# Other handover times, another hold-back rule and two other costs in the planner that orders a fused LSH-attention and expert-network kernel

## The chip, the cores and the metric

The kernel runs on one core of a Trainium2 chip. A core has five engines that run side by side, each working through its own list of instructions in the order in which they were written: TensorE (PE; its weight loads are shown as PEld), VectorE (DVE), ScalarE (ACT), GpSimd (POOL) and SyncE (SP), which here only issues transfers (DMAs). An engine waits when its next instruction needs something that another engine or a transfer has not delivered, and everything behind that instruction waits too. The metric is the time of one execution on the device in microseconds (us).

## The reference

Two stages follow each other. The first is attention in which a query may see only those keys that fall into the same hash bucket; the second is a dense two-layer network with a squared ReLU.

```python
# 4 batches, 8 heads, 768 positions, head size 64
q_bits = einsum(q, proj) > 0                 # 6 bits a row; the same for k
mask   = bucket(q)[:, None] == bucket(k)[None, :]
scores = where(mask, q @ k.T / 8, -1e9)
attn   = exp(scores - max); attn = attn / (sum(attn) + 1e-9)
x      = (attn @ v) as rows of 512           # heads side by side, 3072 rows
h      = x @ w_in                            # 512 -> 2048
out    = (s * relu(h)**2 + b) @ w_out        # 2048 -> 512
```

Everything is in float32, so the kernel splits operands of the matmuls into a high and a low part and adds the products.

## The kernel before, in words

The attention is cut into 96 *slots*: one batch, one head, one chunk of 256 queries against all 768 keys. Batch 0 is visited twice (first chunk 0 of all heads, then chunks 1 and 2); from batch 1 on each head is visited once, with its three chunks. Scores lie transposed, keys on the partitions, in three banks of PSUM, the memory that TensorE writes (128 keys by 256 queries twice in a bank).

A slot has a chain in which each step needs the one before:

- `scores`, first half: score matmuls in pairs (L523 for the exact slots at the start, L525 for all others), the maximum over keys on VectorE (L530, tile `mx`), two transposes on TensorE (L534), a second maximum on VectorE (L536, tile `nmt`), a transpose to rows on TensorE (L538), and the rows made into an operand on VectorE (L544, tile `bq` or `zhl`);
- `scores`, second half: the remaining matmuls, which also subtract the maximum (L553 or L555), and three exponentials on ScalarE (L560). Each exponential frees a bank, into which the next slot's score matmuls go.

Off that chain are `values` (cast and low part of the exponentials on ScalarE and GpSimd, L577 and L578; the matmuls with v, L584 and L585, or L582 in batch 0; the sum over keys on VectorE, L606; for every second head a reciprocal on VectorE, L622, the division on GpSimd, L623, and a transfer of the pair's result `xsb` to DRAM, `xd`, L627), the preparation of a head's queries and keys (L384 to L420), and, in the first part of the kernel, `decode`, which turns 32 blocks of the weights into split float32 (L303 to L316). VectorE's part of a decode are L306 and L307, one dependent on the other.

The second stage is `moe`: 12 chunks of 256 rows. A chunk reads its rows back (`xc<-xd`, L647), four head pairs each; then for each two of 16 blocks of the hidden size there are 24 matmuls (L660), ScalarE and GpSimd steps (L665 to L668), and 12 matmuls with w_out (L677). A chunk has 192 L660 and 96 L677 matmuls. They have the lowest priority, so they fill TensorE between the steps of the attention, earlier chunks ahead of later ones. What is left when attention ends is run alone.

None of this is emitted in program order. Every step is entered into `Plan` (L32) with its engine, an estimated cost, a priority (lower is more urgent) and what it reads and writes. `order` then plays the program through once, before anything is built: it goes from decision to decision, always for the engine that can start soonest; that engine takes, among the steps whose producers have all been placed (`open_`), the most urgent one that is ready. A step is ready when its last producer's cost and *handover time* (`HOP`; less `SAME` where both are on one engine) are over. With `LOOK` an engine may also take a more urgent step that is not ready yet but soon will be, and stays idle until then. The times that come out of this are used for one thing alone: sorted by them, the steps are emitted, and this fixes the order on each engine and on the queues. What is put down as a step's cost changes nothing in the step.

A step's priority is `pr`: slot i has 10 i; the next slot's scores are entered with 10 (i + 1) - 8, exponentials 4 less than that, values 10 i + 5, decodes 10 i + 15, the reciprocal 10 i + 25, the expert network 10000 and more. In `order`, `moved` stands for a transfer queue that moves 260,000 bytes per us.

Of the kernel before, what the change touches and what calls it, by code (L numbers as in the profile page):

```python
# [15 lines left out]
ALU = mybir.AluOpType  # L16
# [11 lines left out]
PE, DVE, ACT, POOL, SP = (mybir.EngineType.PE, mybir.EngineType.DVE, mybir.EngineType.Activation,  # L28
                          mybir.EngineType.Pool, mybir.EngineType.SP)


class Plan:  # L32
# [25 lines left out]
    def order(self):  # L58
        n = len(self.steps)
        left = [len(s[5]) for s in self.steps]  # L60
        users = [[] for _ in range(n)]
        for i, s in enumerate(self.steps):
            for d in s[5]:
                users[d].append(i)
        ready = [0.0] * n
        free = {}
        moved = 0.0
        open_ = {}
        for i in range(n):
            if not left[i]:  # L70
                open_.setdefault(self.steps[i][0], []).append(i)
        out = []
        while len(out) < n:
            best = None
            for e, lst in open_.items():
                if lst:
                    t = max(free.get(e, 0.0), min(ready[i] for i in lst))
                    if best is None or t < best[0]:
                        best = (t, e)
            t, e = best  # L80
            i = min((i for i in open_[e] if ready[i] <= t + LOOK.get(e, 0.0)), key=lambda i: (self.steps[i][3], i))
            open_[e].remove(i)
            eng, cost, fn, pr, lag, deps = self.steps[i]
            start = max(free.get(e, 0.0), ready[i])
            free[e] = start + cost
            end = start + cost + HOP[e]
            if e == SP:
                moved = max(moved, start + cost) + lag
                end += moved - start - cost
            else:  # L90
                end += lag
            out.append((start, i))
            for u in users[i]:
                ready[u] = max(ready[u], end - (SAME[e] if self.steps[u][0] == e else 0.0))
                left[u] -= 1
                if not left[u]:
                    open_.setdefault(self.steps[u][0], []).append(u)
        self.length = max(free.values())
        self.start = {i: t for t, i in out}
        return [i for _, i in sorted(out)]  # L100

HOP = {None: 0.0, PE: 0.2, DVE: 0.13, ACT: 0.2, POOL: 0.1, SP: 1.8}
SAME = {None: 0.0, PE: 0.2, DVE: 0.0, ACT: 0.05, POOL: 0.0, SP: 0.0}
LOOK = {PE: 0.0, DVE: 0.5, ACT: 0.2}


@with_exitstack
def lsh_attention_moe(ctx: ExitStack, tc, q, k, v, proj, w_in, w_out, s, b, out):  # L110
    nc = tc.nc
# [25 lines left out]
    def f32(ap):  # L137
        return ap.bitcast(F32)
# [11 lines left out]
    def dve(n, fn, r, w, pr, ns=None):  # L150
        plan.add(DVE, ((n + 64) / 960.0 if ns is None else ns), fn, r, w, pr)

    def act(n, fn, r, w, pr, more=0.0):
        plan.add(ACT, 0.13 + n / 1070.0 + more, fn, r, w, pr)

    def pool(n, fn, r, w, pr, ns=None):
        plan.add(POOL, (0.12 + n / 430.0 if ns is None else ns), fn, r, w, pr)
# [126 lines left out]
    def decode(u, pr):  # L284
        src, key = dec[u]
        box = {}

        def new():
            box["t"] = wk.tile([P, 512, 2], I32, tag=f"w{u}", name=f"raw{u}")

        def swap():
            wt[key] = wk.tile([P, 2, 512], F32R, tag=f"w{u}", name=f"w{u}")

        def raw():
            return box["t"]
        rk, wk_ = [("raw", u)], [key + (0,), key + (1,)]
        g, gk = osb[:, u % 2, :], ("os", u % 2)
        gi = g.bitcast(I32)

        x = f"e{(u - 16) // 2}"  # L300
        plan.add(None, 0.0, new, [], rk + ([] if u < 16 else AK(x) if u % 2 == 0 else KK(x)) + [("vs", x, u % 2)], pr - 5)

        plan.add(ACT, 0.1, lambda: nc.scalar.dma_start(raw(), src.rearrange("p (n t) -> p n t", t=2)), KK("e0") if u < PACE else [], rk + [("pace", u % PACE)], pr - 5, 5.0)  # L303
        act(512, lambda: nc.scalar.activation(g, raw()[:, :, 1].bitcast(F32), AF.Copy, scale=float(2.0**-112)), rk + [("pace", u % PACE)], [gk], pr)
        act(512, lambda: nc.scalar.activation(raw()[:, :, 0], raw()[:, :, 0].bitcast(U32), AF.Copy, scale=float(2.0**-29)), rk, rk, pr)
        dve(256, lambda: nc.vector.tensor_scalar(raw()[:, :, 1], gi, -2**31, None, ALU.bitwise_and), [gk], rk, pr, 0.54)  # L306
        dve(512, lambda: nc.vector.scalar_tensor_tensor(gi, gi, 3, raw()[:, :, 1], ALU.logical_shift_left, ALU.bitwise_or), rk, [gk], pr, 0.88)  # L307
        pool(512, lambda: nc.gpsimd.tensor_tensor(gi, gi, raw()[:, :, 0], ALU.add), rk, [gk], pr)
        plan.add(None, 0.0, swap, [], rk + wk_, pr)
        act(512, lambda: nc.scalar.copy(wt[key][:, 0], g), [gk], [key + (0,)], pr)  # L310
        if key[0] == "wo":
            if key[1] == 0:
                pool(512, lambda: nc.gpsimd.tensor_copy(bcs, g), [gk], ["bcs"], pr + 5)
            else:
                pool(512, lambda: nc.gpsimd.tensor_tensor(bcs, bcs, g, ALU.add), [gk], ["bcs"], pr + 5)
        pool(512, lambda: nc.gpsimd.tensor_tensor(wt[key][:, 1], g, f32(wt[key][:, 0]), ALU.subtract), [gk, key + (0,)], [key + (1,)], pr)  # L316
# [9 lines left out]
    def AK(x, r=(0, 1), g=(0, 1, 2)):  # L326
        return [("aq", x, i, j) for i in r for j in g]
# [4 lines left out]
    def KK(x, r=(0, 1, 2, 3, 4)):  # L332
        return [("ks", x, i) for i in r]
# [384 lines left out]
    for i in range(NSL):  # L718
        pr = 10.0 * i
# [15 lines left out]
        while nd[0] < min(ND, decodes(i)):  # L735
            decode(nd[0], pr + 15)
            nd[0] += 1
# [58 lines left out]
```

## Time and profile before

| | us |
|---|---|
| median of 3 runs (1116.52 to 1120.74) | 1117.24 |
| the profiled execution | 1122.19 |
| its span, first to last instruction | 1120.4 |
| TensorE busy in it | 1061.0 |
| ScalarE, GpSimd, VectorE busy | 702.5, 683.9, 657.1 |

The profile is of one execution. "Busy" is the time in which an engine had an instruction in work; matmuls are pipelined and their ends are modelled. A row of a group reads: line, engine, operation, tiles out<-in, shapes, count | busy us, mean ns of one | idle time of the engine just before these instructions, and what ended it. In the timeline a piece is: start, length, engine, line, and in square brackets the idle time before it and who ended it. A row of a stretch gives, after its bounds and length, the busy time of each engine with the number of its instructions, then the clock that TensorE was granted (1.00 is full), the share of time in which the DMA engines were busy, and GB/s.

### The profile page before, as it was taken

Reading aid. Unit: us, or ns where it says so; the run is one execution under the profiler, and the core shown is the slowest. Engines: PE = TensorE matmul, PEld = TensorE weight load, DVE = VectorE, ACT = ScalarE, POOL = GpSimd, SP = SyncE. Lnnn points to the kernel's source line nnn. Section 1 sums busy time; section 2 is a strip of 40 time slices with the busy share of each in tenths; the row PEclk is TensorE's granted clock in tenths of the full one; section 3 lists DMA queues with packets and bytes.
Section 4 is the critical chain, followed back from the end, with each engine's and each line's share of the span. In section 5 each row is a group of like instructions: output and inputs, shape, how many; then the busy total and the mean of one; then the engine's idle time right before and its main releaser. Section 6 shows DMA issues by size and latency. Waiting matters only on the chain.

```text
span 1120.4 us, 18819 instructions
## 1 busy us (share of the span) xinstructions
PE 1061.0 (95%) x6862; PEld 919.1 (82%) x6862; DVE 657.1 (59%) x807; ACT 702.5 (63%) x1377; POOL 683.9 (61%) x617
## 2 busy tenths in 40 slices
PE   8998788999999999989999999999999999999998
PEld 6665666878888888778888888888888998898987
DVE  6666576766767776766777676767776752000000
ACT  5556677766677667666767667677776765333332
POOL 5345898876777667656767676767676765222221
PEclk9888899999999999989999999999999999999999
DMA  8644454433322422332333242233233202101010
GB/s 173 160 138 129 131 138 113 131 96 86 89 73 69 133 61 73 90 88 56 78 100 91 53 130 61 76 81 98 63 81 86 70 1 85 39 19 57 1 57 19
DMA packets 99404, 94.49 MB, mean 84 GB/s; under 512 B 68528, under 2 KB 72112, under 8 KB 99312
## 3 DMA queue, kind: packets, MB, share of 16 engines
q1 hardware_dynamic: 94112, 76.24, 26.1%
q10 hardware_dynamic: 5200, 17.05, 5.0%
q8 instruction: 54, 0.88, 0.3%
q14 instruction: 38, 0.31, 0.1%
HBM read 49.81 MB, written 18.87 MB: 61 GB/s over the span
## 4 chain that ended last, share of the span: by engine, by line
PE 80%; DVE 7%; ACT 5%; DMA 3%; POOL 3%; issue 2%; SPq 0%; DVEq 0%; ACTq 0%; POOLq 0%
PE bank L660 23%; PE bank L677 21%; PE bank L555 5%; PE bank L525 5%; PE bank L582 4%; PE bank L585 4%; PE bank L584 4%; PE bank L523 2%; PE bank L534 2%; PE bank L384 2%; PE bank L612 2%; DVE mx L530 2%; DMA xd<-xsb 2%; DMA xc<-xd 1%; ACT et L560 1%
## 5 line engine op out<-in xcount | busy, mean ns | idle before, releaser
L578 POOL TENSOR_TENSOR hl<-et,hl 128x512 fp32r<-128x512 f32 x216 | 278.1, 1317 | 163.0 <-ACT hl L577 147.6
L660 PE MATMUL bank<-xc,w 128*128 128x256 f32 x2304 | 344.8, 288 | 9.5 <-DMA xc<-xd 8.0
L660 PEld LDWEIGHTS bank<-xc,w 128*128 128x128 f32 x2304 | 307.5, 191 | 20.9 <-DMA xc<-xd 9.3
L677 PE MATMUL bank<-w,ghb 128*128 128x512 f32 x768 | 256.3, 397 | 0.0
L668 POOL TENSOR_TENSOR glb<-rb,ghb 128x512 fp32r<-128x512 f32 x96 | 124.4, 1296 | 137.9 <-ACT ghb L667 130.0
L530 DVE TENSOR_REDUCE mx<-bank 128x256 f32<-128x1536 f32 x96 | 168.1, 1752 | 44.0 <-PE bank L525 25.7
L677 PE MATMUL bank<-w,glb 128*128 128x512 f32 x384 | 152.1, 400 | 0.5 <-POOL glb L668 0.5
L665 ACT ACTIVATE rb<-bank 128x512 f32<-128x512 f32 x96 | 57.1, 595 | 151.3 <-PE bank L660 148.7
L677 PEld LDWEIGHTS bank<-w,ghb 128*128 128x128 f32 x768 | 136.7, 189 | 17.2
L560 ACT ACTIVATE et<-bank 128x512 f32<-128x512 f32 x240 | 130.7, 624 | 31.2 <-PE bank L555 27.6
L606 DVE TENSOR_REDUCE zb<-et 128x256 f32<-128x1536 f32 x72 | 126.1, 1751 | 41.3 <-ACT et L560 41.0
L577 ACT CAST hl<-et 128x512 fp32r<-128x512 f32 x216 | 128.6, 661 | 0.8
L584 PE MATMUL bank<-hl,vs 128*128 128x256 f32 x432 | 121.6, 299 | 0.5 <-ACT hl L577 0.5
L525 PE MATMUL bank<-aq,ks 78*128 78x256 f32 x528 | 118.6, 308 | 1.4 <-ACT et L560 0.7
L585 PE MATMUL bank<-hl,vs 128*128 128x256 f32 x432 | 115.8, 288 | 2.9 <-POOL hl L578 2.5
L525 PEld LDWEIGHTS bank<-aq,ks 78*128 78x128 f32 x528 | 91.0, 194 | 12.6 <-ACT ex L560 2.0
L685 DVE SCALAR_TENSOR_TENSOR osb<-bank,misc,bcs 128x512 f32<-128x512 f32 x22 | 16.2, 744 | 132.4 <-PE bank L677 132.4
L585 PEld LDWEIGHTS bank<-hl,vs 128*128 128x128 f32 x432 | 82.5, 191 | 8.8 <-POOL hl L578 6.0
L555 PE MATMUL bank<-bq,ks 128*128 128x256 f32 x528 | 79.5, 287 | 9.6 <-DVE bq L544 8.3
L616 ACT ACTIVATE xpb<-bank,vmn 64x256 f32<-64x256 f32 x96 | 44.9, 468 | 69.3 <-PE bank L585 67.7
L584 PEld LDWEIGHTS bank<-hl,vs 128*128 128x128 f32 x432 | 82.1, 190 | 3.8 <-ACT hl L577 0.7
L622 DVE RECIPROCAL zpb<-zpb 128x256 f32<-128x256 f32 x48 | 83.7, 1743 | 2.3 <-ACT zpb L614 1.9
(111 smaller groups left out, 1662.9 us busy)
## 6 DMA issues: line engine op xcount, KB each, us to landing
xd<-xsb SPq DMA_DIRECT2D x48, 256.0 KB
xc<-xd SPq DMA_DIRECT2D x48, 256.0 KB
raw<-in_moe_w_in_dram ACTq DMA_DIRECT2D x16, 512.0 KB
raw<-in_moe_w_out_dram ACTq DMA_DIRECT2D x16, 512.0 KB
nat<-in_q_dram SPq DMA_DIRECT2D x32, 192.0 KB
nat<-in_k_dram SPq DMA_DIRECT2D x32, 192.0 KB
bq<-aq SPq DMA_DIRECT2D x32, 192.0 KB
out_dram<-osb SPq DMA_DIRECT2D x22, 256.0 KB
```

The lines of the kernel that those rows point to most:

```text
L525: nc.tensor.matmul(o, ks[0:HR + TPC, 0, kt], aq[0:HR + TPC, cs], start=m == 0, stop=m == 1, skip_group_check=True)
L530: dve(S * TPC, lambda: nc.vector.tensor_reduce(t, sc, AX.XY, ALU.max), [("b", b) for b in pb], [tk], pr, 1.75)
L555: nc.tensor.matmul(o, ks[:, 1, kt], bq[:, cs], start=False, stop=m == 1, skip_group_check=True)
L560: act(512, lambda p=p, z=z: nc.scalar.activation(et(z) if plain(i) else pairs(z), bank[:, pb[p]] if plain(i) else bank[:, pb[p]].rearrange ...
L577: act(512, lambda z=z, y=y: nc.scalar.copy(HL[2 * y].rearrange("p (m n) -> p m n", n=CH), pairs(z)), [("e", z)], [("hl", 2 * y)], pr)
L578: pool(512, lambda z=z, y=y: nc.gpsimd.tensor_tensor(HL[2 * y + 1].rearrange("p (m n) -> p m n", n=CH), pairs(z), f32(HL[2 * y]).rearrange ...
L584: nc.tensor.matmul(av, VS[w % 2][:, kt], HL[2 * y][:, ms], start=(kt == 0), stop=False)
L585: nc.tensor.matmul(av, VS[w % 2][:, kt], HL[2 * y + 1][:, ms], start=False, stop=(kt == NT - 1))
L606: dve(S * TPC, lambda: nc.vector.tensor_reduce(ZB, es, AX.XY, ALU.add), [("e", z) for z in range(NE)], ["zb"], pr, 1.75)
L660: nc.tensor.matmul(hp, wt[("wi", n, cc)][:, m % 2, fs], xc[:, m // 2, :], start=(cc == 0 and m == 0), stop=(cc == NC_ - 1 and m == 2))
L668: pool(2 * CH, lambda r=r, gh=gh, gl=gl: nc.gpsimd.tensor_tensor(gl, r, f32(gh), ALU.subtract), [rk, hk], [lk], MP)
L677: nc.tensor.matmul(bank[:, 6 + t, :], (gh, gh, gl)[n][:, ts], wt[("wo", f)][:, n % 2], start=(f == 0 and n == 0), stop=(f == NF - 1 and n ...
```

## The change

Only the planner's numbers and its rule of choice change; no step is added, removed or given other work.

- `HOP`, the handover time: VectorE 0.13 to 0.06 us, ScalarE 0.2 to 0.06, GpSimd 0.1 to 0.06. TensorE (0.2) and SyncE (1.8) stay.
- `SAME`, what is taken off where producer and user are on one engine, is now equal to `HOP` on these three engines, so that a dependent step follows at once in the plan. Before, 0.13, 0.15 and 0.1 us were left between them.
- `LOOK`: ScalarE's goes from 0.2 to 0. VectorE's stays 0.5 but was a time in us and is now a factor: the most urgent ready step is found first, and a more urgent one is taken in its place only if it will be ready within half the found step's cost.
- VectorE's decode steps are entered with 0.68 and 1.1 us instead of 0.54 and 0.88.

```diff
-            i = min((i for i in open_[e] if ready[i] <= t + LOOK.get(e, 0.0)), key=lambda i: (self.steps[i][3], i))
+            rank = lambda i: (self.steps[i][3], i)
+            i = min((i for i in open_[e] if ready[i] <= t), key=rank)
+            i = min((j for j in open_[e] if ready[j] <= t + LOOK.get(e, 0.0) * self.steps[i][1] and rank(j) <= rank(i)), key=rank)
...
-HOP = {None: 0.0, PE: 0.2, DVE: 0.13, ACT: 0.2, POOL: 0.1, SP: 1.8}
-SAME = {None: 0.0, PE: 0.2, DVE: 0.0, ACT: 0.05, POOL: 0.0, SP: 0.0}
-LOOK = {PE: 0.0, DVE: 0.5, ACT: 0.2}
+HOP = {None: 0.0, PE: 0.2, DVE: 0.06, ACT: 0.06, POOL: 0.06, SP: 1.8}
+SAME = {None: 0.0, PE: 0.2, DVE: 0.06, ACT: 0.06, POOL: 0.06, SP: 0.0}
+LOOK = {DVE: 0.5, ACT: 0.0, POOL: 0.0}
...
-        dve(256, lambda: nc.vector.tensor_scalar(raw()[:, :, 1], gi, -2**31, None, ALU.bitwise_and), [gk], rk, pr, 0.54)
-        dve(512, lambda: nc.vector.scalar_tensor_tensor(gi, gi, 3, raw()[:, :, 1], ALU.logical_shift_left, ALU.bitwise_or), rk, [gk], pr, 0.88)
+        dve(256, lambda: nc.vector.tensor_scalar(raw()[:, :, 1], gi, -2**31, None, ALU.bitwise_and), [gk], rk, pr, 0.68)
+        dve(512, lambda: nc.vector.scalar_tensor_tensor(gi, gi, 3, raw()[:, :, 1], ALU.logical_shift_left, ALU.bitwise_or), rk, [gk], pr, 1.1)
```

## The prediction

> **What bounds the kernel now.** I read the page first: its engine rows, the granted clock in 40 slices, and the chain that ended last.
>
> ```profile
> span 1120.4 us, 18819 instructions
> PE 1061.0 (95%) x6862; PEld 919.1 (82%) x6862; DVE 657.1 (59%) x807; ACT 702.5 (63%) x1377; POOL 683.9 (61%) x617
> ...
> PEclk9888899999999999989999999999999999999999
> ...
> PE 80%; DVE 7%; ACT 5%; DMA 3%; POOL 3%; issue 2%; SPq 0%; DVEq 0%; ACTq 0%; POOLq 0%
> ```
>
> TensorE is busy for 1061.0 of 1120.4 us. The change adds and removes no instruction, so it can only act on the other 59 us, and on the slices in which the granted clock is below 9. Next, the stretches: busy time of each engine, granted clock, DMA share.
>
> ```profile
> core 0: us, PE busy (x) PEld busy (x) DVE busy (x) ACT busy (x) POOL busy (x), PEclk, DMA share, GB/s
> 84.00:224.00 140.00, 116.15 (x608) 92.95 (x607) 94.72 (x104) 98.50 (x186) 113.00 (x92) 0.93 0.45 129
> 224.00:470.00 246.00, 235.83 (x1619) 208.99 (x1618) 174.42 (x211) 171.41 (x348) 169.15 (x156) 1.00 0.33 85
> 470.00:486.00 16.00, 10.35 (x57) 8.63 (x56) 9.25 (x12) 6.79 (x15) 6.92 (x7) 0.79 0.27 70
> 486.00:905.00 419.00, 408.58 (x2844) 365.25 (x2845) 300.24 (x351) 298.71 (x603) 294.25 (x274) 1.00 0.31 80
> 905.00:1121.00 216.00, 210.68 (x1346) 189.62 (x1344) 25.61 (x30) 79.87 (x137) 64.72 (x55) 1.00 0.11 36
> ```
>
> TensorE's idle time is 23.9 us in 84 to 224 (140 - 116.15), 10.2 in 224 to 470, 5.7 in 470 to 486, 10.4 in 486 to 905, 5.3 in the last stretch. That last stretch is nothing but expert-network matmuls that were left over. So attention that finishes earlier does not end the kernel earlier by itself: filler that is no longer run between its steps is run in the tail. The end moves by TensorE's idle and half-clock time alone.
>
> Does attention from 486 on wait for TensorE, or TensorE for attention? These are groups of that stretch; the last columns are idle time before the group and what ended it.
>
> ```profile
> L606 DVE TENSOR_REDUCE zb<-et 128x256 f32<-128x1536 f32 x45 | 78.8, 1751 | 22.3 <-ACT et L560 22.2
> L585 PE MATMUL bank<-hl,vs 128*128 128x256 f32 x266 | 71.4, 288 | 1.4 <-POOL hl L578 1.2
> L555 PE MATMUL bank<-bq,ks 128*128 128x256 f32 x264 | 38.5, 282 | 0.0
> L544 DVE SCALAR_TENSOR_TENSOR bq<-bank,ident 2x256 fp32r<-2x256 f32 x44 | 18.1, 412 | 38.1 <-PE bank L538 38.1
> L538 PE MATMUL bank<-ident,nmt 128*2 128x128 f32 x44 | 11.9, 271 | 3.0 <-ACT aq L386 3.0
> ```
>
> VectorE waits 38.1 us for the row transposes (L538), TensorE 0.0 us for what VectorE then makes of them (L555). The chain's results lie ready and wait for their turn in TensorE's written order. There the order decides, and the handover times hardly do.
>
> **The change, part by part.**
>
> *Handover times.* The planner's time from an engine's end to another's start goes to 0.06 us for VectorE (from 0.13), ScalarE (0.2) and GpSimd (0.1). What the trace has, where TensorE did stand waiting:
>
> ```profile
> 128.52 0.41 DVE L544 SCALAR_TENSOR_TENSOR bq<-bank,ident 2x256 fp32r<-2x256 f32 x1 [0.36 <-PE bank L538]
> 128.98 0.98 PE L555 MATMUL bank<-bq,ks 128*128 128x256 f32 x6 [0.51 <-DVE bq L544]
> ...
> 400.35 0.47 ACT L386 ACTIVATE aq<-bank,misc 128x256 fp32r<-128x256 f32 x1 [1.85 <-DVE nmt L536]
> 400.88 0.27 PE L538 MATMUL bank<-ident,nmt 128*2 128x128 f32 x1 [0.55 <-ACT aq L386]
> ```
>
> 128.52 + 0.41 = 128.93 to 128.98 is 0.05 us; 400.82 to 400.88 is 0.06. The new figures are right. A slot's chain has three handovers from VectorE (L530, L536, L544) and one from ScalarE (exponential to the next slot's scores): 3 x 0.07 + 0.14 = 0.35 us less per slot in the plan. TensorE's written order then has up to 0.35 us less filler between the chain steps of a slot. From 486 to 905 the trace has 45 slots (L606), 9.3 us each, so some 26 lie between 224 and 470; over those it is up to 9 us of filler not yet used when batch 1's attention ends. On the end itself: 0, by the last stretch above, except at one place, next.
>
> *The batch boundary at 470 to 486.* Filler of batch 0 is three chunks of 192 L660 matmuls, 576. The trace, L660 alone and then pieces of the timeline:
>
> ```profile
> 0.00:472.40 472.40, 97.48 (x585) 81.40 (x585) 0.95 0.42 111
> 472.40:481.10 8.70, 0.00 (x0) 0.00 (x0) 0.81 0.40 100
> ```
>
> ```profile
> 470.28 0.38 SPq L145 DMA_DIRECT2D xd<-xsb  x1
> ...
> 477.00 0.41 DVE L544 SCALAR_TENSOR_TENSOR bq<-bank,ident 2x256 fp32r<-2x256 f32 x1 [0.36 <-PE bank L538]
> ...
> 478.46 0.33 SPq L647 DMA_DIRECT2D xc<-xd  x1
> ...
> 481.15 0.58 PE L660 MATMUL bank<-xc,w 128*128 128x256 f32 x1 [4.18 <-DMA xc<-xd]
> ...
> 482.38 1.48 PE L555 MATMUL bank<-bq,ks 128*128 128x256 f32 x6
> ```
>
> At 472.4 all 576 are done, and 9 of batch 1 (its first three head pairs). The next L660 needs the fourth pair. The planner gives a transfer 0.7 us of issue, 1 us of moving and 1.8 of handover; the write to DRAM issued at 470.28 lets its read start only at 478.46. So TensorE stands 4.18 us at an L660, and the chain's L555, whose input was ready at 477.41, waits behind it until 482.38. Then the clock:
>
> ```profile
> 477.74:484.57 6.83, 3.42 (x16) 3.42 (x17) 1.32 (x3) 1.88 (x4) 1.71 (x2) 0.50 0.23 70
> 191.02:194.44 3.42, 3.42 (x12) 2.87 (x11) 0.23 (x1) 3.19 (x7) 3.42 (x3) 0.50 0.60 170
> 675.72:679.13 3.41, 2.88 (x13) 2.88 (x14) 2.35 (x3) 2.20 (x5) 3.41 (x4) 0.50 0.31 68
> ```
>
> Work that took 3.42 us at 0.50 would take 1.71 at full clock. If filler of batch 0 is left, it comes first (earlier chunks have the higher priority) and the stall is covered. Worth: 5.65 us idle in the stretch, less 0.4 that 16 us of the stretch after would have anyway (10.42 / 419 x 16), plus 1.7 for the clock: 7.0 us. Bounds: 0 (nothing left over) to 7.0. I take 7.0: some 4 us of leftover covers the 4.2 us stall, and up to 9 is offered.
>
> The rows at 191 and 675 show the clock halved by lesser stalls as well. The Trainium skill, "TensorE: Matmul & The Clock Gate", section "Why this matters for your kernels", advises against idle gaps over about 3 us, because an idle window of that length throttles the array. By that rule a new gap of 1 to 2 us would cost its own length. This trace has the half clock at 675.72, where no gap reached 3 us, so by the rows it can cost up to 1.7 us on top (half of 3.4).
>
> *Margins.* The old figures were longer than the hardware's, and so were a cushion. Where TensorE meets its producer exactly, each error of the plan now becomes a stall. From 486 on little of that is in sight (L555 0.0, L585 1.4, L538 3.0 us over 44 slots). Bounds: 0, and a doubling of the idle time from 224 to 470 and 486 to 905, +20.6. I take +1.5, near L585's 1.4, since results there wait for TensorE. The freed cushion is near the lower bound.
>
> *Holding back.* Before, an idle VectorE waited up to 0.5 us for a step of higher rank, whatever it held back. Now it waits up to half the cost of that operation: 0.875 us for 1.75 us ones, 0.55 for the second decode step, 0.34 for the first, 0.21 to 0.27 for the short ones. But the planner sees a step only once all its producers are placed, and it places the engine that can start soonest first. A step behind TensorE is therefore seen at most a TensorE cost and handover ahead: 0.43 us for L536 (0.23 + 0.2), 0.32 for L544, 0.44 for an inexact slot's L530. All are below the old 0.5. For long operations the new bound holds back nothing more there, only before steps behind an exponential (0.61 + 0.06) and behind the long exact score groups; for short ones it holds back less. And right at the end of L530, L534 is not yet placed, so L536 is not seen at all. What this costs today, in 84 to 224:
>
> ```profile
> 115.11 1.76 DVE L530 TENSOR_REDUCE mx<-bank 128x256 f32<-128x1536 f32 x1 [1.50 <-PE bank L525]
> 116.79 1.74 DVE L622 RECIPROCAL zpb<-zpb 128x256 f32<-128x256 f32 x1
> 118.45 0.36 DVE L536 TENSOR_REDUCE nmt<-bank 128x2 f32<-128x256 f32 x1
> 118.73 1.26 DVE L306 TENSOR_SCALAR raw<-osb 128x512 int32<-128x512 int32 x1
> 119.91 0.41 DVE L544 SCALAR_TENSOR_TENSOR bq<-bank,ident 2x256 fp32r<-2x256 f32 x1
> ...
> 118.87 0.27 PE L538 MATMUL bank<-ident,nmt 128*2 128x128 f32 x1 [1.44 <-DVE nmt L536]
> 120.37 1.01 PE L555 MATMUL bank<-bq,ks 128*128 128x256 f32 x3 [1.23 <-DVE bq L544]
> ```
>
> A reciprocal straight after L530 costs TensorE 1.44 us, a decode step straight after L536 costs 1.23. By the code above, both can come again. ScalarE no longer waits at all (0.2 before): an exponential may then start behind another operation, and what waits for it is the next slot's scores and L606 on VectorE. That lengthens a slot; TensorE has filler meanwhile, so 0, and without filler up to one ScalarE operation in such a slot. The stage in sum:
>
> ```profile
> L530 DVE TENSOR_REDUCE mx<-bank 128x256 f32<-128x1536 f32 x16 | 28.0, 1753 | 26.9 <-PE bank L525 22.5 <-ACT raw L305 3.5 <-PE bank L523 1.0
> L555 PE MATMUL bank<-bq,ks 128*128 128x256 f32 x81 | 13.6, 305 | 9.1 <-DVE bq L544 7.8 <-POOL bq L433 1.2
> ```
>
> 16 slots, in which TensorE waits 7.8 us for L544. At best 70% of that goes, 5.5 us, and two halved windows of 1.7: -9. At worst as much comes: +9. I take -1, nearer nothing than either, since the mechanism stays and only some cost figures come closer.
>
> *Decode costs* go to 0.68 and 1.1 us.
>
> ```profile
> L307 DVE SCALAR_TENSOR_TENSOR osb<-osb,raw 128x512 int32<-128x512 int32 x32 | 37.0, 1157 | 0.5
> L306 DVE TENSOR_SCALAR raw<-osb 128x512 int32<-128x512 int32 x32 | 21.7, 679 | 3.8 <-ACT osb L304 3.7
> ```
>
> The means agree. The plan gives VectorE 32 x 0.36 = 11.5 us more, the chip does the same work: 0. But one figure stands for different things (1.26 us at 118.73 against a mean of 0.68). The Trainium skill, "SBUF — State Buffer", names a port pair that VectorE and GpSimd take exclusively, the loser blocked for a whole instruction. By it a decode step in front of the chain costs what GpSimd's running instruction has left, which the plan does not hold.
>
> *Sum:* -7.0 + 1.5 - 1 = -6.5 us. The profiled execution took 1122.19 us, 1.8 more than its span and 4.95 more than the median of the runs shown, 1117.24; the terms are differences, so I put them to the median: 1110.7, say 1110.5 us.
>
> **The rivals.**
>
> *The boundary stays (chance 0.22).* The real slot is set by TensorE's order and by VectorE's 1.75 us blocks, and does not shorten by the plan's 0.35 us; filler runs out as before. For it: 9 of batch 1's matmuls were done already, so there was no margin at all. Then the small terms alone: 1117.24 + 0.5, 1117.7 us.
>
> *Decode steps block the chain more often (0.24): slower.* L306 and L307 now follow each other without the 0.13 us between dependent VectorE steps, and short ones are held back less. Place: 84 to 224, with little filler to cover. Price: about 1.2 us per slot (the 1.23 above); the 7.8 us of today are worth six or seven such stalls in 16 slots. Seven more are +8.4 us, one more halved window +1.7, with the boundary as before: about 1127. It decides from five more on (6 us).
>
> *The hold works where it is needed (0.14).* If the plan's new times move the reciprocals and decode steps out of those places, the lower bound above comes true, -9 in place of -1, beside the boundary: 1117.24 - 7.0 + 1.5 - 9 = 1102.7, say 1102. Against it: the planner's blindness just after L530 and L536.
>
> *My forecast (0.40):* the boundary is covered, 1106 to 1114.
>
> **How the numbers follow.** A measurement here tells about 0.5% from no change, 5.6 us: faster is under 1111.7, slower over 1122.8. Faster: 0.8 of 0.40, nearly all of 0.14, a little of the first rival: 0.47. Same: most of the first rival, and 0.07 of my case: 0.28. Slower: 0.25. The range runs from just below the case of the working hold, 1099, to the slower case's price at 1127.
>
> **What would show it.** Right: no 4 us idle before L660 near the end of batch 1, no halved window behind it, attention's last slot some 10 to 25 us earlier (0.35 x 72 slots) and a tail longer by as much; idle time before L585 and L538 a little up. Wrong: that stall still there; or TensorE's idle time in 84 to 224 off 23.9 us by more than 5 either way; or a new idle time of several us elsewhere, such as behind a read of xc at another chunk.

## The result, and the profile after

The changed kernel takes 1125.59 us (median of 5 runs, 1123.23 to 1128.45); the kernel before, run beside it on the same chip, takes 1116.61. The ratio is 1.0077, 95% interval 1.0051 to 1.0102: some 9 us slower. I had forecast 1110.5 us, faster. (In the changed file all lines behind the new rule are 2 higher: L530 is now L532, L544 is L546, L555 is L557, L660 is L662.)

The page of the kernel after, in the rows shown of before:

```profile
span 1126.7 us, 18822 instructions
PE 1063.8 (94%) x6862; PEld 918.7 (82%) x6862; DVE 655.9 (58%) x807; ACT 700.5 (62%) x1377; POOL 683.4 (61%) x617
PEclk8888989899999999999999999999999999999999
PE 67%; DVE 4%; ACT 3%; issue 3%; POOL 3%; DMA 2%; SPq 0%; ACTq 0%; DVEq 0%; POOLq 0%
```

TensorE's work is the same 6862 matmuls. The last row cannot be compared with the 80% of before as it stands: the closing chain of the kernel after is followed back only to 199.83 us, 82% of the span, and TensorE has 67 of these 82. The stretches of the kernel after (bounds and length; busy time per engine; granted clock; DMA):

```profile
84.00:224.00 140.00, 111.42 (x565) 88.70 (x564) 89.86 (x99) 91.61 (x174) 103.25 (x84) 0.88 0.45 125
224.00:470.00 246.00, 235.41 (x1613) 206.87 (x1612) 175.59 (x210) 172.01 (x352) 169.95 (x156) 1.00 0.32 83
470.00:486.00 16.00, 14.90 (x102) 12.73 (x100) 10.83 (x15) 10.18 (x20) 12.59 (x13) 1.00 0.43 121
486.00:905.00 419.00, 406.77 (x2818) 362.30 (x2819) 302.09 (x354) 296.74 (x602) 294.47 (x274) 1.00 0.31 80
905.00:1127.00 222.00, 216.96 (x1388) 195.41 (x1386) 24.82 (x28) 81.31 (x140) 64.83 (x55) 1.00 0.10 35
```

The batch boundary did what the forecast said: in 470 to 486 TensorE is idle for 1.1 us (16 - 14.90) in place of 5.65, at full clock in place of 0.79. But 84 to 224 has 28.6 us of idle time in place of 23.9, at 0.88 in place of 0.93, and 43 matmuls fewer (565, 608).

To see both sides apart, I cut each execution where the same slot, the 23rd, takes its first maximum: its L530 starts at 226.98 us before, its L532 at 235.99 after. The stretches up to there and behind it, first of the kernel before, then of the kernel after:

```profile
0.00:227.01 227.01, 198.56 (x1022) 149.35 (x1023) 149.56 (x208) 148.53 (x282) 151.23 (x129) 0.90 0.51 138
227.01:1120.40 893.39, 862.43 (x5842) 769.74 (x5840) 507.53 (x600) 553.96 (x1096) 532.70 (x489) 0.99 0.27 71
```

```profile
0.00:236.02 236.02, 198.95 (x999) 148.61 (x1000) 148.21 (x209) 147.96 (x283) 150.47 (x130) 0.88 0.50 135
236.02:1126.70 890.68, 864.81 (x5865) 770.09 (x5863) 507.72 (x599) 552.54 (x1096) 532.92 (x488) 1.00 0.26 70
```

That point is reached 9.0 us later, with 23 matmuls fewer done. Idle time up to it: 28.45 before, 37.07 after, +8.6; behind it 30.96 and 25.87, -5.1. At half clock TensorE loses half of the time in which it is busy; half clock during idle time costs nothing on top. By the traces' clock records TensorE was busy at half clock for 43.2 us before and 51.1 after up to that point, 6.3 and 3.4 behind it: +4.0 and -1.4. Together some 12.6 us were lost early and 6.5 won later, +6.0; the span grew by 6.3. (The other way of counting agrees: 9.0 us, and 23 matmuls at the mean of 1061.0 / 6862 = 0.155 us, make 12.6.)

The largest new piece of idle time, in three views of the kernel after: the timeline; the waits of the sequencers of ScalarE for L388 (`split`'s scale) and of VectorE for L546, in ns; and the stretch at half clock.

```profile
193.17 0.57 SPq L147 DMA_DIRECT2D aq<-bq  x1
...
202.60 0.47 ACT L388 ACTIVATE aq<-bank,misc 128x256 fp32r<-128x256 f32 x1 [6.08 <-issue]
203.17 0.41 DVE L546 SCALAR_TENSOR_TENSOR bq<-bank,ident 2x256 fp32r<-2x256 f32 x1 [5.70 <-issue]
...
203.68 1.62 PE L557 MATMUL bank<-bq,ks 128*128 128x256 f32 x6 [6.48 <-DVE bq L546]
```

```profile
L388 ACTq EVENT_SEMAPHORE  x1: 7127/7127/7127, 195.4 to 195.4; - x1
...
L546 DVEq EVENT_SEMAPHORE  x1: 6534/6534/6534, 196.6 to 196.6; - x1
```

```profile
198.90:209.10 10.20, 5.42 (x19) 4.90 (x20) 1.84 (x4) 3.05 (x6) 3.49 (x3) 0.50 0.09 22
```

L388 belongs to the first split of batch 1's first head and waits for a 6 KB copy into `aq`. The copy was issued at 193.17; L388's wait ends at 195.4 + 7.1 = 202.5, and the trace's last count on the copy's semaphore is at 202.53. That is 9.4 us, where the plan has 0.7 + 0.02 + 1.8 = 2.5. So the planner took L388 for ready at about 195.7 and put it ahead of the chain step L546. L546 shares no data with it: it reads the row in the first half of PSUM bank 4, L388 the turned queries in the second half. Yet in the built program L546 waits for ScalarE's count: its wait ends at 196.6 + 6.5 = 203.1, when L388 ends (202.60 + 0.47). TensorE stands for 6.48 us, from 197.2 to 203.7. Half clock sets in at 198.9, within that gap, and lasts for 10.2 us; TensorE is busy for 5.42 of them, which costs it 2.7 us more. The Trainium skill, "PSUM — Partial Sum Buffer", section "PSUM bank collisions raise a hardware error ⚠️", says that two engines must not touch one bank and partition group at the same time, reads against reads included, and that software orders them. The trace agrees with such an order; the plan has separate keys for the two halves and does not know of it.

In the kernel before the step stands one slot further back, ahead of the next slot's L544:

```profile
197.37 0.57 SPq L145 DMA_DIRECT2D aq<-bq  x1
...
205.74 0.47 ACT L386 ACTIVATE aq<-bank,misc 128x256 fp32r<-128x256 f32 x1 [0.24 <-PE bank L538]
```

8.4 us after the copy's issue it waits no more. A second new stall, also in the kernel after, has the same pattern with another step:

```profile
227.80 0.41 ACT L626 CAST xsb<-xpb 128x256 fp32r<-128x256 f32 x1 [3.66 <-DMA xd<-xsb]
...
228.60 0.65 ACT L306 ACTIVATE osb<-raw 128x512 f32<-128x512 f32 x1
229.28 1.26 DVE L308 TENSOR_SCALAR raw<-osb 128x512 int32<-128x512 int32 x1 [2.36 <-ACT osb L306]
230.46 0.41 DVE L538 TENSOR_REDUCE nmt<-bank 128x2 f32<-128x256 f32 x1
230.93 0.27 PE L540 MATMUL bank<-ident,nmt 128*2 128x128 f32 x1 [2.57 <-DVE nmt L538]
```

ScalarE waits for a transfer out of `xsb`, the decode's L306 stands behind it, VectorE's L308 behind L306, and the chain's L538 behind L308.

### The profile page after: what moved, and what is told of

It is laid out like the page before. It is cut to its first block, busy times and chain, and to the rows that moved or that the text cites. A ratio compares the mean times of both kernels' runs of the same rounds, so it can differ in the third digit from the quotient of the medians.

```text
span 1126.7 us, 18822 instructions
## 1 busy us (share of the span) xinstructions
PE 1063.8 (94%) x6862; PEld 918.7 (82%) x6862; DVE 655.9 (58%) x807; ACT 700.5 (62%) x1377; POOL 683.4 (61%) x617
## 4 chain that ended last, share of the span: by engine, by line
PE 67%; DVE 4%; ACT 3%; issue 3%; POOL 3%; DMA 2%; SPq 0%; ACTq 0%; DVEq 0%; POOLq 0%
PE bank L662 21%; PE bank L679 20%; PE bank L557 5%; PE bank L527 4%; PE bank L587 4%; PE bank L586 4%; PE bank L536 2%; PE bank L614 2%; PE bank L386 2%; POOL hl L580 2%; DMA xd<-xsb 1%; PE bank L411 1%; PE bank L540 1%; ACT aq L388 1%; DVE nmt L538 1%
## 5 line engine op out<-in xcount | busy, mean ns | idle before, releaser
L662 PE MATMUL bank<-xc,w 128*128 128x256 f32 x2304 | 338.4, 286 | 6.8 <-DMA xc<-xd 5.7
L662 PEld LDWEIGHTS bank<-xc,w 128*128 128x128 f32 x2304 | 305.4, 189 | 17.1 <-DMA xc<-xd 3.4
L532 DVE TENSOR_REDUCE mx<-bank 128x256 f32<-128x1536 f32 x96 | 168.0, 1750 | 49.2 <-PE bank L527 30.2
L527 PE MATMUL bank<-aq,ks 78*128 78x256 f32 x528 | 122.6, 316 | 2.1 <-ACT ex L562 1.5
L586 PE MATMUL bank<-hl,vs 128*128 128x256 f32 x432 | 119.7, 295 | 0.0
L587 PE MATMUL bank<-hl,vs 128*128 128x256 f32 x432 | 114.7, 286 | 1.1 <-POOL hl L580 0.8
L557 PE MATMUL bank<-bq,ks 128*128 128x256 f32 x528 | 82.3, 292 | 11.5 <-DVE bq L546 11.5
L587 PEld LDWEIGHTS bank<-hl,vs 128*128 128x128 f32 x432 | 81.9, 189 | 7.7 <-POOL hl L580 4.5
L557 PEld LDWEIGHTS bank<-bq,ks 128*128 128x128 f32 x528 | 70.5, 192 | 17.3 <-DVE bq L546 8.8
```

The costliest lines, as they stand in the source:

```text
L527: nc.tensor.matmul(o, ks[0:HR + TPC, 0, kt], aq[0:HR + TPC, cs], start=m == 0, stop=m == 1, skip_group_check=True)
L532: dve(S * TPC, lambda: nc.vector.tensor_reduce(t, sc, AX.XY, ALU.max), [("b", b) for b in pb], [tk], pr, 1.75)
L557: nc.tensor.matmul(o, ks[:, 1, kt], bq[:, cs], start=False, stop=m == 1, skip_group_check=True)
L586: nc.tensor.matmul(av, VS[w % 2][:, kt], HL[2 * y][:, ms], start=(kt == 0), stop=False)
L587: nc.tensor.matmul(av, VS[w % 2][:, kt], HL[2 * y + 1][:, ms], start=False, stop=(kt == NT - 1))
L662: nc.tensor.matmul(hp, wt[("wi", n, cc)][:, m % 2, fs], xc[:, m // 2, :], start=(cc == 0 and m == 0), stop=(cc == NC_ - 1 and m == 2))
```

## The experiments

Three theories. **W**: the order is what costs; which step that waits for a transfer comes out ahead of the chain in the early stage is a matter of chance, and any edit of the planner's figures draws anew. **C**: the cushion; shorter handover times cost time by themselves. **H**: the hold rule and the decode costs. Every ratio is to the kernel before, run beside it on the same chip, with its 95% interval.

**One part alone.** The diff of `e1_hop_only` is the change's `HOP` and `SAME` lines, of `e2_look_only` its rule and `LOOK`, of `e3_cost_only` its two decode costs; each on the kernel before.

> The kernel before with the new handover times alone (HOP and SAME). Theory W (a waiting step in front of the chain): the 9 us are lost between 84 and 236, where a step that waits for a transfer happens to stand ahead of a chain step in an engine's written order; the parts of the change only reshuffle that order. By W no part has the loss as such: this kernel may land anywhere from -6 to +9 us against before, and its time is explained to 2 us by TensorE's idle and half-clock time before 240. Theory C (the cushion is gone): the shorter handover times themselves cost, in many small stalls; this kernel alone is 6 to 9 us slower, with idle time after 486 up from 10.4 us by several us. Theory H (the hold and the costs): this kernel is within 3 us of before or faster.

> The kernel before with the new rule of holding back alone. W: anywhere from -6 to +9 us, explained by idle and half-clock time before 240. C: within 3 us of before. H: 5 to 9 us slower, with TensorE waiting longer for L544 and L536 in 84 to 224 (7.8 and some 5 us before) in many waits of about 1.2 us, since short operations are no longer held back.

> The kernel before with the two new decode costs alone. W: anywhere from -6 to +9 us. C: within 3 us of before. H: some us slower, through decode steps ahead of the chain in 84 to 224. After 300, where no decode is left, this kernel's order should be nearly that of before by all theories.

Measured: handovers alone 1.0141 (1.0109 to 1.0173), the rule alone 1.0018 (0.9990 to 1.0045), the costs alone 0.9995 (0.9973 to 1.0017). H falls as a cause by itself; the handover times alone are even slower than the whole change. C and W both allow that, but C had also put the loss into many small stalls, with idle time after 486 up by several us: from 486 to 905 it is 10.6 us in `e1_hop_only`, against 10.4 before. W's finer forecast, that idle and half-clock time before 240 explain the time of `e1_hop_only` to 2 us, was off by little: they give 6.3 of the 8.5 us by which its span is longer.

**The waiting step moved.** `e4_move_split` keeps the changed kernel's order except for three steps: turn (L386), scale (L388) and rest (L389) of that first split come just before the second split's. (`MOVED` holds the place of each split's first step; the lines that fill it are left out here.)

```diff
...
+    late = [MOVED[0] + x for x in range(3)]
+    queue = [i for i in queue if i not in late]
+    at = queue.index(MOVED[1])
+    queue[at:at] = late
```

> The changed kernel with three steps moved in the written order, nothing else: the first split of batch 1's first head (transposes L386, ScalarE's copy L388, VectorE's L389) goes to just before that head's second split. In the changed kernel ScalarE's L388 waits 7.1 us for transfers, and the chain's L546 stands behind it, so that TensorE idles 6.48 us at 197 and runs at half clock from 198.9 to 209.1. W: that stall goes, with most of the 10.2 us at half clock (worth 5): 1114 to 1120 us, about as before. If the chain waits there for something else as well (C, H, or the transfer itself, since L388 is needed two slots later): the stall shrinks to some 3 us or comes one slot later, and the time stays over 1122.

Measured: 1.0001 (0.9979 to 1.0023), 0.0076 better than the changed kernel, and level with the kernel before. Before the same L557 TensorE now waits for 1.62 us:

```profile
193.91 0.95 PE L557 MATMUL bank<-bq,ks 128*128 128x256 f32 x6 [1.62 <-DVE bq L546]
```

By the starts of the maxima in the two profiled executions, three slots across this place (from the 18th to the 21st) take 25.1 us in place of 30.4: by these two traces the move is worth 5.3 us at its place. The 18th starts 5.5 us earlier as well: 3.0 of that is there by the seventh, ahead of every moved step (the first, the turn, stood at 90.7 in TensorE's order), the rest comes up to the 16th, where the order lacks nothing but the turn. More than half of the 5.5 is half-clock time, and what brings it is not shown.

**One part left out.** `e5_no_hop` is the change without its handovers, `e6_no_look` without its rule, `e7_no_cost` without its decode costs.

> The changed kernel with the old handover times (HOP and SAME as before), the new hold rule and the new decode costs kept. Theory C (the shorter handover times cost, since the handover times alone gave +14 us): within 4 us of before. Theory W (a chance order: any new order can put a waiting step ahead of the chain in the early stage): -6 to +15 us, with no relation to which part is in.

> The new handover times and decode costs, with the old hold rule. C: 6 to 16 us slower than before, as with the handover times alone. W: -6 to +15 us, not related to e1.

> The new handover times and hold rule, with the old decode costs. C: 6 to 16 us slower than before. W: -6 to +15 us.

Measured: 0.9966 (0.9947 to 0.9986), 1.0094 (1.0065 to 1.0122), 0.9951 (0.9931 to 0.9971). The second is as C said. The last speaks against C: it has the short handovers and beats the kernel before. And the parts do not add. Decode costs alone gave -0.0005, but put on the pair of handovers and rule they take it from 0.9951 to 1.0077, +0.0126. The three single effects add up to +0.0154; together they measure +0.0077.

**Handovers longer than before.**

```diff
-HOP = {None: 0.0, PE: 0.2, DVE: 0.13, ACT: 0.2, POOL: 0.1, SP: 1.8}
-SAME = {None: 0.0, PE: 0.2, DVE: 0.0, ACT: 0.05, POOL: 0.0, SP: 0.0}
+HOP = {None: 0.0, PE: 0.2, DVE: 0.2, ACT: 0.34, POOL: 0.14, SP: 1.8}
+SAME = {None: 0.0, PE: 0.2, DVE: 0.07, ACT: 0.19, POOL: 0.04, SP: 0.0}
```

> The kernel before with handover times between engines made longer by as much as the change made them shorter (VectorE 0.2, ScalarE 0.34, GpSimd 0.14 us; what is left between dependent steps of one engine as before). C, if more cushion means fewer stalls: 0 to 8 us faster than before, with less TensorE idle time before 240. W: -6 to +15 us with stalls of another pattern.

> The hold rule as changed together with handovers between engines longer than before (0.20, 0.34 and 0.14 us for VectorE, ScalarE and GpSimd, within the engine 0.13, 0.15 and 0.10 as in the run with longer handovers), decode costs as before. Theory C (cushion: long handover times help, short ones cost): the two gains add, 0.992 to 0.995, since the longer handovers alone gave 0.9945 and the rule alone 1.002. Theory W: the parts do not add; any ratio from 0.993 to 1.008.

Measured: longer handovers alone 0.9945 (0.9920 to 0.9970); with the hold rule (`e12_more_look`) 1.0027 (1.0008 to 1.0046). The rule cost nothing measurable by itself and 0.008 here. C, by which the two gains would add to 0.992 to 0.995, falls.

**One hundredth of a microsecond.** The changed kernel with 0.07 (`e9_hop_07`) and 0.05 (`e10_hop_05`) for its 0.06 in both tables; and the kernel before with 0.01 more between engines (`e16_before_01`).

> The changed kernel with 0.07 us in place of 0.06 in both tables for VectorE, ScalarE and GpSimd; everything else as changed. One hundredth of a microsecond has no meaning of its own, but the order comes out in other places. Theory W (chance: which step that waits for a transfer comes out ahead of the attention chain in the early stage): the time moves by several us, most likely back towards the kernel before, 1112 to 1124, and the stall of 6.48 us before L557 at 197 is not there or stands elsewhere. Theory C (the shorter handover times themselves cost the time, whatever their exact figure): as the changed kernel, ratio 1.006 to 1.010 to the kernel before.

> The changed kernel with 0.05 us in place of 0.06. Theory W: another time again, anywhere from 1110 to 1130, and not on a line with the one for 0.07; the two of them and the changed kernel are spread over at least 5 us. Theory C: as the changed kernel, ratio 1.006 to 1.010, and if it follows the size, a little slower than with 0.07.

> The kernel before with its handovers between engines longer by one hundredth of a microsecond (0.14, 0.21, 0.11; within an engine as before). Theory W in its wide form (any small edit of the plan's figures moves the time by several us through the order): off the kernel before by 0.3% or more in either direction. If the kernel before were a tuned point that any edit of handovers leaves for the worse: 1.004 to 1.010. If small edits do little about the old figures: 0.998 to 1.002.

Measured: 0.9904 (0.9868 to 0.9939) with 0.07, 1.0095 (1.0062 to 1.0127) with 0.05, 1.0036 (1.0014 to 1.0059) for the kernel before with 0.01 more. The first two lie just outside the ranges that W had given (1112 to 1124 and 1110 to 1130), one on each side; the third is 0.36% off, little more than the 0.3% that W asked for, and nearly what an edit of a tuned point would give. So figures that differ by 0.02 us, and mean the same, give times 21 us apart (1110.63 and 1131.62); the kernel with 0.07 is the fastest of this study and beats both kernels. This is W's clearest point: the changed kernel lies between the two. With 0.05 the old place is back, shown by its timeline:

```profile
185.63 0.57 SPq L147 DMA_DIRECT2D aq<-bq  x1
...
194.72 0.47 ACT L388 ACTIVATE aq<-bank,misc 128x256 fp32r<-128x256 f32 x1 [4.12 <-issue]
195.28 0.41 DVE L546 SCALAR_TENSOR_TENSOR bq<-bank,ident 2x256 fp32r<-2x256 f32 x1 [3.84 <-issue]
...
195.79 1.62 PE L557 MATMUL bank<-bq,ks 128*128 128x256 f32 x6 [5.64 <-DVE bq L546]
```

With 0.07 L388 waits for the copy too, but it comes out between two chain steps at which nothing on TensorE waits for it (timeline, then the stretch, in which TensorE is idle for 16.8 us):

```profile
184.73 0.57 SPq L147 DMA_DIRECT2D aq<-bq  x1
...
187.14 0.95 PE L557 MATMUL bank<-bq,ks 128*128 128x256 f32 x6 [0.61 <-DVE bq L546]
...
191.56 0.47 ACT L388 ACTIVATE aq<-bank,misc 128x256 fp32r<-128x256 f32 x1 [2.25 <-issue]
```

```profile
84.00:224.00 140.00, 123.20 (x669) 99.99 (x668) 95.49 (x107) 100.82 (x192) 112.85 (x91) 0.94 0.46 138
```

**A plan that counts transfers longer.** The changed kernel with 6.0 in place of 1.8 us for SyncE in `HOP`.

> The changed kernel with one figure altered: the planner counts 6.0 us in place of 1.8 from the end of a transfer's issue to its data (the copy that caused the 6.48 us stall took 9.36 us). Theory W in its narrow form (the planner places steps too early because it takes transfers for short): the steps that wait for a transfer come out later, no idle of over 4 us before L557 in 84 to 224, idle time of TensorE in that stage down from 28.6 to 20 to 25, ratio to the kernel before 0.990 to 0.998. If it is only chance which step comes out where: any ratio from 0.994 to 1.010, with stalls in other places. Theory C: 1.006 to 1.010, since the handover times stand as changed.

Measured: 1.0082 (1.0050 to 1.0113). W in its narrow form, that the plan need only count transfers longer, fails. The large stall at 197 is gone and TensorE's idle time in 84 to 224 is down to 19.4 us, as that form said, but the loss turns up elsewhere, most plainly at the batch boundary:

```profile
84.00:224.00 140.00, 120.63 (x660) 97.82 (x659) 99.46 (x105) 98.15 (x189) 113.87 (x92) 0.94 0.45 126
224.00:470.00 246.00, 231.41 (x1549) 204.97 (x1548) 169.81 (x206) 162.54 (x330) 160.10 (x149) 0.97 0.31 83
470.00:486.00 16.00, 10.52 (x51) 8.78 (x49) 10.54 (x12) 9.81 (x21) 9.50 (x11) 0.61 0.29 81
```

14.6 us idle in 224 to 470 (10.6 in the kernel after), and 5.5 us idle at a clock of 0.61 in 470 to 486.

**The same move in three other orders.** Is that one step the cause wherever a stall stands behind it? `e13_05_move`, `e14_more_move` and `e15_nohop_move` are `e10_hop_05`, `e12_more_look` and `e5_no_hop` with the lines of `e4_move_split`. In the second of them, `e12_more_look`, the profile names the whole row of waits, the copy included:

```profile
209.97 0.47 ACT L388 ACTIVATE aq<-bank,misc 128x256 fp32r<-128x256 f32 x1 [4.00 <-DMA aq<-bq]
...
210.50 0.37 PE L540 MATMUL bank<-ident,nmt 128*2 128x128 f32 x1 [4.85 <-ACT aq L388]
```

Here even TensorE's transpose into the first half of bank 4 waits for ScalarE's read of the second half.

> The kernel with 0.05 us handovers (1.0095), whose order is kept but for three steps: the turn, scale and rest of the first split of batch 1's first head, which wait for the copy into aq and stand ahead of the chain, come just before the second split's. In that kernel TensorE stood 5.64 us at 190.15 before L557 behind the same ScalarE instruction, and half clock followed from 194.5 for 6.8 us. Theory W with this one step as the cause: 5.64 + 3.4 = 9.0 us less, ratio to the kernel before 1.001 (0.999 to 1.005). If the step is only where lost time shows and not its cause: the stall comes back at the next step that waits for that copy, ratio 1.006 to 1.010.

> The kernel with longer handovers and the hold rule (1.0027), order kept but for the same three steps. There TensorE stood 4.85 us at 205.64 before L540 <- ACT aq L388, the same copy, and half clock followed from 210.1 for 6.8 us. W with this step as the cause: 4.85 + 3.4 = 8.3 us less, ratio 0.9953 (0.993 to 0.999). If the stall only comes back elsewhere: 1.001 to 1.005.

> The kernel with the hold rule and the decode costs but the handovers of before (0.9966), order kept but for the same three steps. There TensorE stood 4.42 us at 191.12 before L540 <- ACT aq L388 and half clock followed from 193.8 for 6.8 us. W with this step as the cause: 4.42 + 3.4 = 7.8 us less, ratio 0.990 (0.987 to 0.994), as good as the best order so far (0.9904). If the stall only comes back elsewhere: 0.995 to 0.999.

| order | without the move | with it | 18th to 21st maximum, us |
|---|---|---|---|
| changed kernel | 1.0077 (1.0051 to 1.0102) | 1.0001 (0.9979 to 1.0023) | 30.4 to 25.1 |
| 0.05 us | 1.0095 (1.0062 to 1.0127) | 1.0063 (1.0037 to 1.0088) | 30.4 to 26.2 |
| long handovers and rule | 1.0027 (1.0008 to 1.0046) | 1.0043 (1.0019 to 1.0066) | 33.0 to 31.3 |
| rule and costs | 0.9966 (0.9947 to 0.9986) | 0.9956 (0.9929 to 0.9983) | 32.8 to 32.3 |

(The last column is from the starts of the maxima in the traces.) I had expected 7.8 to 9.0 us in each of the three. (These sums priced all 6.8 us of half clock behind each stall; TensorE was busy for 5.5, 5.9 and 4.5 of them, so they were 0.5 to 1.2 us too high.) All three medians fall into the range that I had put down for a stall that comes back elsewhere. The stall itself goes in all, down to 1.6 to 1.7 us before the chain's next matmul, but what that wins is 4.2 us in one order and 1.7 and 0.5 in the others. There the moved steps make waits of their own, as in `e15_nohop_move`:

```profile
193.85 1.42 PE L557 MATMUL bank<-bq,ks 128*128 128x256 f32 x6 [1.69 <-DVE bq L546]
...
196.32 0.49 DVE L389 SCALAR_TENSOR_TENSOR bq<-bank,misc,aq 128x256 fp32r<-128x256 f32 x1 [2.23 <-ACT aq L388]
...
196.86 0.69 PE L386 MATMUL bank<-ident,nat 128*128 128x128 f32 x2 [1.16 <-DVE bq L389]
```

The second split's turn stands in TensorE's order right behind the first split's last step, and waits for it. So this one step is shown as the largest single loss of the changed kernel, about 5 of its 9 us by the traces (0.0076, 8.5 us, by the medians); as a general cause it is not.

**All orders together.** The planner made 14 different orders of the same work (all kernels but the four with moved steps). Their ratios run from 0.9904 to 1.0141; six are slower than 1.003 and four faster than 0.997, and the standard deviation of the 14 is 0.0068, 7.6 us. The kernel before lies in the middle of them, and the changed kernel is an ordinary one. Nor does the early stage alone decide: `e16_before_01`, with the most idle time in 84 to 224, measured 1.0036, and `e11_sp_late`, with 9 us less than the changed kernel, 1.0082.

## Why the prediction was wrong

**Handover figures (right, as read from VectorE and ScalarE).** The changed kernel's trace has 0.05 us from VectorE to TensorE, 189.71 + 0.41 = 190.12 to 190.17:

```profile
189.71 0.41 DVE L546 SCALAR_TENSOR_TENSOR bq<-bank,ident 2x256 fp32r<-2x256 f32 x1 [0.36 <-PE bank L540]
...
190.17 0.98 PE L557 MATMUL bank<-bq,ks 128*128 128x256 f32 x6 [0.50 <-DVE bq L546]
```

That a figure comes nearer to the hardware did not make the order better.

**Shorter slots, 0 on the end (the time right, the reason not shown).** The last slot's maximum starts at 916.84, at 920.22 before; from the 23rd to the last it is 680.9 us in place of 693.2, so 12.4 us shorter, in the forecast's 10 to 25. The tail has more matmuls for it (1388 against 1346 from 905 on). But that the handovers did it is not shown: this stretch takes 694.2 us in `e6_no_look`, which has the new ones, and 684.1 in `e5_no_hop`, which has the old.

**The batch boundary, -7.0 (the size right, in part by luck).** The stretch's idle time fell from 5.65 to 1.10 us and its half clock went: 4.55 and, at the forecast's price for the clock, 1.7, so 6.3. The mechanism is there too: the last of batch 0's 576 filler matmuls starts at 473.3, at 458.0 before, so batch 1's were needed later. But it does not follow from the handovers. At this place TensorE's wait for `xc`, 4.18 us before and 1.10 after, is 3.1 us in `e7_no_cost` and 2.7 in `e6_no_look`, both with the new handovers, none in `e1_hop_only`, and 1.9 in `e2_look_only` with the old ones; and `e11_sp_late`, with the same short handovers between the engines, has 5.5 us of idle time in the stretch at a clock of 0.61. It is a property of this order.

**Margins, +1.5 (the sign right, small).** From 486 on:

```profile
L587 PE MATMUL bank<-hl,vs 128*128 128x256 f32 x270 | 72.0, 288 | 0.9 <-POOL hl L580 0.6
L557 PE MATMUL bank<-bq,ks 128*128 128x256 f32 x267 | 41.8, 293 | 0.6 <-DVE bq L546 0.6
L540 PE MATMUL bank<-ident,nmt 128*2 128x128 f32 x45 | 12.2, 271 | 2.7 <-ACT aq L388 1.8 <-DVE nmt L538 1.0
```

L587 and L540 wait no longer than before (1.4 and 3.0), L557 0.6 in place of 0.0. In 224 to 470 the idle time rose by 0.4 us (10.6 against 10.2), in 486 to 905 by 1.8 (12.2 against 10.4). The latter is no eroded margin but one stall behind a read of `xc`, the kind that the forecast named as possible at another chunk (timeline, then the stretch behind it):

```profile
765.31 0.62 PE L662 MATMUL bank<-xc,w 128*128 128x256 f32 x2 [2.83 <-DMA xc<-xd]
```

```profile
765.50:768.90 3.40, 3.40 (x17) 3.40 (x17) 0.54 (x1) 1.66 (x3) 1.28 (x2) 0.50 0.02 9
```

**Holding back, -1 (this is the step that failed).** It was the only term that the sum had for 84 to 224, with bounds of -9 and +9, and its mechanism was decode steps and reciprocals in front of the chain. Up to the 23rd slot 12.6 us more were lost than before in the profiled executions, only 0.8 of them ahead of 84. The other 11.7, 7.5 of idle time and 4.2 at half clock, lie outside the bounds; 84 to 224 by itself has 4.7 and 4.2, which is the upper bound. My own sign for this, 5 us more idle in 84 to 224, looked at idle time alone and just missed it. The new rule, whose effect the step priced, measured 1.0018 alone. What the step left out: every step of the stage is re-sorted, not only those that the new rule touches; a copy takes 7 to 9 us there where the plan has 2.5; and bank 4 ties steps together that the plan takes for independent. It took the old order's losses there (23.9 us idle) as given, plus or minus a few stalls. They are one draw: the 14 orders have from 15.5 us of idle time in this stretch (`e8_hop_more`) to 30.1 (`e16_before_01`).

**Decode costs, 0.** Alone 0.9995, as said; put on top of the other two, +0.0126. No sum of terms holds such a figure.

**The rival that ended slower** had the right place (84 to 224), and its 1127 us is near the 1125.59 measured, but its mechanism is not what the trace shows as the main thing. TensorE's waits for the chain's two VectorE steps in that stretch of the kernel after, and the second of them before:

```profile
L557 PE MATMUL bank<-bq,ks 128*128 128x256 f32 x78 | 12.9, 303 | 10.6 <-DVE bq L546 10.6
L540 PE MATMUL bank<-ident,nmt 128*2 128x128 f32 x15 | 4.1, 271 | 5.7 <-DVE nmt L538 5.7
```

```profile
L538 PE MATMUL bank<-ident,nmt 128*2 128x128 f32 x16 | 4.3, 271 | 5.1 <-DVE nmt L536 5.0
```

10.6 us for L546 against 7.8, of which 6.48 is the one stall behind the copy, and 5.7 for L538 against 5.0. Without that stall 9.8 us are left for the two, fewer than the 12.8 of before: there are no seven further stalls of 1.2.

**The Trainium skill's rule** of the 3 us gap, under "TensorE: Matmul & The Clock Gate", "Why this matters for your kernels": the 10.2 us of half clock at 198.9 fit it only roughly, since they set in 1.7 us after TensorE fell idle (it had stood for 1.4 us just before). The row at 765.50 followed a gap of 2.83 us, near that figure. Stretches of half clock with far smaller gaps ahead of them stand at the end of this document.

## What to carry to other kernels

Where one pass of a greedy planner fixes an order, an edit of its figures is first of all a new draw: before you credit or blame the edit, measure how far the time moves for edits that mean nothing (here 0.01 us), and do not forecast a gain smaller than that from the terms you can name. It also means that trying a dozen nearby figures and keeping the best order is cheap: the best of 14 measured 0.9904 here (0.9868 to 0.9939; as the pick of many it may flatter a little). In the trace, look for a chain step that stands behind another engine's wait for a transfer without sharing its data: a PSUM bank used by both for different things is enough.

## What the runs showed that I had not expected

**Half clock that TensorE's gaps do not explain.** `e10_hop_05` and `e13_05_move` have the same order up to the first moved step, which stands at 85 in the first. Stretches of the first, then of the second:

```profile
53.50:57.00 3.50, 3.50 (x25) 2.42 (x24) 2.88 (x7) 1.99 (x4) 0.72 (x1) 0.85 0.72 225
...
60.00:70.00 10.00, 10.00 (x51) 6.87 (x50) 7.09 (x11) 7.44 (x15) 7.32 (x7) 1.00 0.34 91
```

```profile
53.50:57.00 3.50, 2.42 (x15) 1.41 (x14) 3.36 (x6) 1.27 (x3) 1.45 (x2) 1.00 0.46 117
57.00:60.40 3.40, 3.40 (x30) 2.36 (x28) 3.33 (x5) 3.33 (x8) 2.30 (x2) 0.99 0.72 220
...
60.40:70.60 10.20, 10.20 (x25) 5.99 (x24) 4.43 (x7) 4.14 (x8) 5.00 (x5) 0.50 0.28 86
```

Only the second has a gap, 1.08 us, and some 5 us behind it TensorE ran for 10.2 us at half clock, busy all the while: about 5 us lost, with no other gap between (57.00 to 60.40 is all busy). That the gap brings it is not shown. The kernel before has such a stretch with no gap over 0.5 us in the 25 us ahead of it:

```profile
68.14:78.38 10.24, 10.24 (x24) 6.09 (x24) 4.81 (x6) 3.44 (x8) 1.45 (x2) 0.50 0.43 137
```

So idle time of TensorE alone does not tell where the clock falls; what does stays open. Where the same order can lose 5 us in one execution and not in another, two profiled executions are not enough to price an edit of that size; the medians of several runs are the better measure.

**A 6 KB copy took 9.4 us** (up to the start of L388 9.1 with 0.05 us, 6.8 with 0.07), beside transfers of up to 512 KB issued around it. Whether those make it so slow wasn't tried.
